# Two layers of linear attention and gated MLP on one core: wider MLP blocks, folded keys for the first tile, and four adjacent tokens to a partition

## The chip, the cores and the metric

The kernel runs on one core of a Trainium2 chip. The metric is the device time of one execution in microseconds, on the slowest core, of which there is one here. The core has five engines that run side by side, each through a fixed sequence of its own: TensorE (PE: matmuls and transposes by matmul; PEld are its weight loads), VectorE (DVE), ScalarE (ACT), GpSimd (POOL) and SyncE (SP, which here only issues transfers). Transfers are carried out by DMA engines that the queues share. Matmuls write to PSUM, everything else lies in SBUF, 128 partitions wide.

## The reference

One sequence of 2048 tokens of width 512 goes twice through the same pair of blocks, with the same weights both times. Type bf16 throughout.

```python
def _A_ref(x, wqkv, w_phi, wo):                      # H = 32 heads of Dh = 16
    qkv = (x @ wqkv).reshape(B, S, 3, H, Dh).transpose(2, 0, 3, 1, 4)
    q, k, v = qkv[0], qkv[1], qkv[2]
    pq = einsum("bhsd,hdf->bhsf", q, w_phi); pk = einsum("bhsd,hdf->bhsf", k, w_phi)
    phi_q = concatenate([softmax(pq), softmax(-pq)]); phi_k = concatenate([softmax(pk), softmax(-pk)])
    kv = einsum("bhsf,bhsd->bhfd", phi_k, v); z = einsum("bhsf->bhf", phi_k)
    o = einsum("bhqf,bhfd->bhqd", phi_q, kv) / (einsum("bhqf,bhf->bhq", phi_q, z)[..., None] + 1e-6)
    return o.transpose(0, 2, 1, 3).reshape(B, S, D) @ wo

def _B_ref(x, W_gate, W_up, W_down):                 # F = 1376
    gate, up = x @ W_gate, x @ W_up
    return ((gate * (gate > 0)) * up) @ W_down

x = A_x
x = x + _A_ref(_layernorm(x), A_wqkv, A_w_phi, A_wo)
x = x + _B_ref(_layernorm(x), B_W_gate, B_W_up, B_W_down)
x = x + _A_ref(_layernorm(x), A_wqkv, A_w_phi, A_wo)
x = x + _B_ref(_layernorm(x), B_W_gate, B_W_up, B_W_down)
```

The sums kv and z run over all tokens, so the queries' part of a layer (`erq` below) cannot begin before the last key of that layer is done.

## The kernel before

**Tiles.** The 2048 tokens are 16 tiles of 128. x stays in SBUF in four chunks X of four tiles each. Token `128 t + p` is on partition p of tile t (`xv` and `ov`, L287 and L288): one partition reads one token, 1 KB, for each tile.

**Start.** ScalarE's queue and SP's queue load x, the key weights wk (into hT_163, in two halves), the value weights wv and the feature weights wf. `chain` (L363) makes each load of a queue follow the one before. Meanwhile nine warm-up matmuls run on TensorE (L445), and one more between two later steps, where IDLE (L173) says so. Since the features of a head are softmax(k wf) with k = x wk, the product wk wf is folded once into Wk2: wcen (VectorE, from wf, L432) and Wblk (a block-diagonal form of it, L433); 16 transposes of wk on TensorE (L471), copied from PSUM to hT_164 (L451 on ScalarE, L452 on VectorE); 16 matmuls with Wblk (L479); four casts into Wk2, 480 columns each (L451, L452). 480 is 32 heads of 15, since the 16th feature follows from the sum.

**Keys and values.** For each tile: statistics on VectorE (L508), a log and an exponential on ScalarE for the deviation (L516, L518), the scaled tile xn (VectorE or GpSimd, L530), a transposition into xnTA (tiles 0 to 3 on TensorE, L498, with a copy at L451 or L452; the others by a transposing transfer that SP issues, L493), then K (four matmuls of 480 columns with Wk2, L600), two exponentials of it (L572), V (four of 512, L605), its copy vext, the sums of the features, their products `ek` (`phi`, VectorE or GpSimd, L559), and the accumulation kvz (L633). With PLAIN = 1 tile 0 takes another path: k = x wk unfolded (KT, 16 matmuls, L591), a copy, then four matmuls with Wblk (L596). It needs neither the transposes of wk nor the folds.

**Queries.** When kvz is complete, VectorE builds R from it (L645, L650). For each tile: Q (L660), exponentials, sums, a ratio, a product `phq` (GpSimd or VectorE, L681) and a transposing transfer fq on SP (L685). `attend` (L690) takes two tiles at a time: erq (eight small matmuls into the one q buffer of PSUM, L696), a reciprocal and the product o on VectorE (L710), the transposing transfer oT on SP (L493), and the output projection (four matmuls of 512, L719), added to x.

**MLP.** `mlp` (L729) works on a block of n tiles: x is centred (xn) and transposed into xnTB by SP (L493). A loop over the ten full f-blocks of 128 makes gate and up, four matmuls each (L796), with n x 128 columns each; narrower blocks take several f-blocks to a PSUM bank (`step = 512 // W`). The last 96 columns of gate and up are made tile by tile (L772) and turned on SP (`hrT`, L823). ScalarE applies the relu (L800); the product hT is made on VectorE, from a copy that ScalarE makes or directly from PSUM. The down projection (L836) has 11 matmuls of 512 columns for each tile; its result is added to x (L843). BLOCKS (L182) gives the widths of the blocks in each layer.

**The order.** Every step is recorded by `op(...)` and runs where a table says: ORDER lists all steps in one sequence, and each engine and each queue runs its own in that sequence; PLACE picks the engine of every step that has two ways (a copy on ScalarE or VectorE, a product on GpSimd or VectorE, a load on SP's or ScalarE's queue); SLOTS names the buffer that each step takes. PSUM has one q buffer and six b buffers. Names such as hT_163 or b_105 are buffers; a number behind the name only tells which.

Of the kernel before, what the change touches and what calls it, by code (L numbers as in the profile page):

```python
# [8 lines left out]
P = 128  # L9
# [136 lines left out]
class K:  # L146
# [9 lines left out]
    "1110001010101011000100001101110100010000110100000001011000010110001111001001000001011100001100001100"  # L156
    "1111010101001111110000100000110110011010010101100000100011000100100000011100111100010000100010111110"
    "1110001011110100001010100000110011100100101001111100101100010101011011111000110100110110100111000100"
    "0010000100011010011111011001000111111100101110100100001"
)  # L160
SLOTS = (
    "0001451040132010500014430222331211020213005544034243050301110131332321832325222114330207421163021150"
    "43375021032559100a020c214d141b332h054f362c105k231i3549013a320g141e203j165b01000000011111020002530110"
    "2052000011050000204202101213001021020100001400010001042032225056210020141101113100001013443103004200"
    "5024102252034024832130232211211001211414305400512015021500501424203120233311431134500254221004105021"
    "02015020100312401021224420100230221701026341142312581332141121113251055111242400k5433334000000400550"
    "4123310521121425400211j0213d222h110f303c033a065k2559325f311d101g145b323g155i002a210c032e260114210204"
    "1100101010020002320110212400001034011022530000104100011021210011114014020514023010050015242135111114"
    "0112013132253124000220001300002341212232511021352150000541521101013132122010250142250053200130123002"
    "05310400520232022520411404202003012523313501311300121120432"  # L170
# [3 lines left out]
    0, 0, 0, 1,  # L174
# [106 lines left out]
def kernel(  # L281
    ctx: ExitStack, tc: tile.TileContext, A_x, A_wqkv, A_w_phi, A_wo, B_x, B_W_gate, B_W_up,
    B_W_down, out):
    nc = tc.nc
    xf, of = A_x.flatten_outer_dims(), out.flatten_outer_dims()
    assert tuple(xf.shape) == (T * P, D)
    xv = xf.rearrange("(t p) d -> p t d", p=P)  # L287
    ov = of.rearrange("(t p) d -> p t d", p=P)  # L288

    sb = ctx.enter_context(tc.tile_pool(name="sb", bufs=1))  # L290
# [72 lines left out]
    def chain(makers):  # L363
        made = []
        for make in makers:
            made.append(make(made[-1:]))
# [588 lines left out]
```

## Time and profile before

| what | value |
|---|---|
| median of 3 runs | 369.92 us (369.61, 369.94, 369.92) |
| the profiled execution's own time | 369.7 us |
| its span, first to last recorded instruction | 367.9 us |
| granted TensorE clock, mean over the span | 1.000 |
| TensorE instructions (matmuls) | 2845 |

The busy shares by slice (40 slices of 9.2 us; 9 means 90% or more) show where each engine works:

```profile
PE   8999999999999999999999999998999999999996
DVE  6999999999886656656799897896874553353415
ACT  5999999343554731356665576863612354212231
POOL 3769931100010000011002172120000000000000
```

The first six slices are the keys of layer 0, with all four engines at work; the keys of layer 1 are made between the MLP blocks of layer 0. The 1.8 us between the span and the execution's time lie outside the recorded instructions.

In the profile's groups of instructions a row reads: line, engine, operation, what it writes <- what it reads, shape, count | busy time, mean ns of one | idle time of the engine just before them, and what ended most of it. In the chain of work that ended last, a row reads: start, length, engine or transfer, buffer, line, count.

### The profile page before, as it was taken

Reading aid. Unit: us, or ns where it says so; the run is one execution under the profiler, and the core shown is the slowest. Engines: PE = TensorE matmul, PEld = TensorE weight load, DVE = VectorE, ACT = ScalarE, POOL = GpSimd, SP = SyncE. Lnnn points to the kernel's source line nnn. Section 1 sums busy time; section 2 is a strip of 40 time slices with the busy share of each in tenths; the row PEclk is TensorE's granted clock in tenths of the full one; section 3 lists DMA queues with packets and bytes.
Section 4 is the critical chain, followed back from the end, with each engine's and each line's share of the span. In section 5 each row is a group of like instructions: output and inputs, shape, how many; then the busy total and the mean of one; then the engine's idle time right before and its main releaser. Section 6 shows DMA issues by size and latency. Waiting matters only on the chain.

```text
span 367.9 us, 7455 instructions
## 1 busy us (share of the span) xinstructions
PE 362.1 (98%) x2845; PEld 217.1 (59%) x2845; DVE 264.5 (72%) x617; ACT 196.6 (53%) x561; POOL 56.6 (15%) x84
## 2 busy tenths in 40 slices
PE   8999999999999999999999999998999999999996
PEld 5455568786554544465767456786654544456674
DVE  6999999999886656656799897896874553353415
ACT  5999999343554731356665576863612354212231
POOL 3769931100010000011002172120000000000000
PEclk9999999999999999999999999999999999999999
DMA  7992983488416302122202350245961220110222
GB/s 229 244 244 64 328 135 61 113 107 178 87 43 116 71 13 18 29 44 58 66 0 66 58 117 7 52 88 78 149 139 25 57 43 2 43 45 0 88 58 87
DMA packets 93924, 31.73 MB, mean 86 GB/s; under 512 B 85344, under 2 KB 92864, under 8 KB 93888
## 3 DMA queue, kind: packets, MB, share of 16 engines
q1 hardware_dynamic: 93616, 31.00, 39.0%
q8 instruction: 22, 0.36, 0.4%
q10 hardware_dynamic: 272, 0.26, 0.2%
q14 instruction: 14, 0.11, 0.1%
HBM read 8.44 MB, written 2.10 MB: 29 GB/s over the span
## 4 chain that ended last, share of the span: by engine, by line
PE 96%; DMA 1%; ACT 1%; DVE 0%; issue 0%
PE b L796 38%; PE b L836 20%; PE b L719 8%; PE b L605 7%; PE b L660 7%; PE b L600 6%; PE b L772 3%; PE q L696 2%; PE q L633 2%; DMA oT<-o 1%; PE q L445 1%; PE b L498 1%; ACT ek L572 1%; PE b L479 0%; PE b L471 0%; DVE X L843 0%
## 5 line engine op out<-in xcount | busy, mean ns | idle before, releaser
L796 PE MATMUL b<-xnTB,wgu 128*128 128x128 bf16 (+2 forms) x1200 | 152.1, 279 | 0.0
L796 PEld LDWEIGHTS <-wgu 128*128 128x128 bf16 x1200 | 97.7, 98 | 46.5
L800 ACT ACTIVATE gu<-b 128x512 bf16<-128x512 f32 (+1 forms) x83 | 47.5, 581 | 93.9 <-PE b L796 85.3
L836 PE MATMUL b<-wd,hT 128*128 128x512 bf16 (+3 forms) x363 | 84.6, 372 | 0.0
L572 ACT ACTIVATE ek<-b 128x480 bf16<-128x480 f32 x128 | 69.4, 587 | 16.2 <-PE b L660 7.7
L813 DVE TENSOR_TENSOR hT<-gu,b 128x512 bf16<-128x512 bf16 (+1 forms) x46 | 30.9, 676 | 33.3 <-PE b L796 19.4
L836 PEld LDWEIGHTS <-hT 128*128 128x128 bf16 (+1 forms) x363 | 34.3, 98 | 33.9
L559 POOL TENSOR_TENSOR ek<-ek 128x480 bf16<-128x480 bf16 x33 | 32.9, 1023 | 127.0 <-ACT sq L670 56.4
L843 DVE SCALAR_TENSOR_TENSOR X<-b,rsB,X 128x512 bf16<-128x512 f32 (+2 forms) x33 | 24.0, 731 | 21.9 <-PE b L836 21.9
L665 DVE TENSOR_REDUCE sq<-ek 128x64 f32<-128x960 bf16 x32 | 36.4, 1143 | 1.3 <-ACT ek L572 1.2
L610 DVE TENSOR_REDUCE sk<-ek 128x64 f32<-128x960 bf16 x32 | 35.8, 1139 | 0.0
L719 PE MATMUL b<-wo,oT 128*128 128x512 bf16 x128 | 31.7, 379 | 1.3 <-DMA oT<-o 1.2
L605 PE MATMUL b<-wv,xnTA 128*128 128x512 bf16 x128 | 31.5, 379 | 0.0
L600 PE MATMUL b<-Wk,xnTA 128*128 128x480 bf16 x124 | 29.5, 366 | 0.6 <-ACT vext L451 0.6
L660 PE MATMUL b<-Wq,xnTA 128*128 128x480 bf16 x128 | 29.7, 366 | 0.0
L804 DVE TENSOR_TENSOR hT<-gu 128x512 bf16<-128x512 bf16 (+1 forms) x37 | 14.8, 401 | 18.0 <-ACT gu L815 17.8
L815 ACT CAST gu<-b 128x512 bf16<-128x512 f32 (+1 forms) x37 | 20.2, 555 | 12.3 <-PE b L796 12.3
L710 DVE TENSOR_TENSOR o<-q,rd 128x512 bf16<-128x512 f32 x32 | 22.0, 687 | 5.8 <-ACT rd L707 5.5
L723 DVE SCALAR_TENSOR_TENSOR X<-b,X 128x512 bf16<-128x512 f32 x32 | 21.8, 684 | 3.8 <-PE b L719 3.6
L508 DVE BATCH_NORM_STATS2 bstA<-X 128x6 f32<-128x512 bf16 x32 | 21.6, 682 | 1.5 <-DMA X<-in_A_x_dram 1.3
L681 POOL TENSOR_TENSOR ek<-ek 128x480 bf16<-128x480 bf16 x13 | 12.9, 994 | 51.3 <-DVE ek L676 48.0
L719 PEld LDWEIGHTS <-oT 128*128 128x128 bf16 x128 | 11.8, 98 | 13.4 <-DMA oT<-o 1.9
(80 smaller groups left out, 339.3 us busy)
## 6 DMA issues: line engine op xcount, KB each, us to landing
out_dram<-X SPq DMA_DIRECT2D x15, 128.0 KB, 1.8
X<-in_A_x_dram SPq DMA_DIRECT2D x6, 256.0 KB, 4.9
wgu<-in_B_W_up_dram SPq DMA_DIRECT2D x4, 344.0 KB, 4.1
wgu<-in_B_W_gate_dram SPq DMA_DIRECT2D x4, 344.0 KB, 5.3
wd<-in_B_W_down_dram SPq DMA_DIRECT2D x5, 256.0 KB, 3.7
hT<-in_A_wqkv_dram SPq DMA_DIRECT2D x3, 256.0 KB, 4.5
X<-in_A_x_dram SPq DMA_DIRECT2D x4, 128.0 KB, 3.3
wv<-in_A_wqkv_dram SPq DMA_DIRECT2D x2, 256.0 KB, 4.8
```

The costliest lines, as they stand in the source:

```text
L559: e.tensor_tensor(out=v[:, :, 0:DF, :], in0=v[:, :, 0:DF, :], in1=spread(ek, v, n), op=Alu.mult)
L572: nc.scalar.activation(out=pairs(ek, s)[:, :, 0:DF, :], in_=ps.t[:, 0:FW].rearrange("p (b f h) -> p b f h", h=2, f=DF), func=AF.Exp, scale ...
L600: k = op("PE", mm(4, FW), due, lambda: [nc.tensor.matmul(kp.t[:, 0:FW], lhsT=xnTA[c][:, i, b, :], rhs=Wk2[:, b, :], start=(b == 0), stop=( ...
L605: v = op("PE", mm(4, 512), due_v, lambda: [nc.tensor.matmul(vp.t[:], lhsT=xnTA[c][:, i, b, :], rhs=wv[:, b, :], start=(b == 0), stop=(b == ...
L610: a = op("DVE", SUM16, due, lambda: nc.vector.tensor_reduce(out=sk.t[:, row, :].rearrange("p (b h) -> p b h", h=2), in_=summed(pairs(ek)), ...
L660: q = op("PE", mm(4, FW), due, lambda: [nc.tensor.matmul(qp.t[:, 0:FW], lhsT=xnTA[c][:, i, b, :], rhs=Wq2[:, b, :], start=(b == 0), stop=( ...
L665: a = op("DVE", SUM16, due, lambda: nc.vector.tensor_reduce(out=sq.t[:].rearrange("p (b h) -> p b h", h=2), in_=summed(pairs(ek)), axis=AX ...
L719: a = op("PE", mm(4, 512), due + 3, lambda j=j, yp=yp: [nc.tensor.matmul(yp.t[:], lhsT=oT.t[:, j, b, :], rhs=wo[:, b, :], start=(b == 0), ...
L796: nc.tensor.matmul(ps.t[:, q * W:(q + 1) * W].rearrange("p (i t) -> p i t", t=P), lhsT=wgu[:, s, b, g * P:(g + 1) * P], rhs=xT.t[:, 0:n, b ...
L800: nc.scalar.activation(out=gu.t[:, 0, 0:cols], in_=gp.t[:, 0:cols], func=AF.Relu)
L813: nc.vector.tensor_tensor(out=h.t[:, f0 * W:f0 * W + cols], in0=gu.t[:, 0, 0:cols], in1=up.t[:, 0:cols], op=Alu.mult)
L836: nc.tensor.matmul(yp.t[:, 0:c1 - c0], lhsT=h.t[:m, f * W + i * P:f * W + (i + 1) * P], rhs=wd[:m, f, c0:c1], start=(f == 0), stop=(f == N ...
```

## The change

Four things change.

- MLP blocks are 1, 1, 2, 4, 4 and 4 tiles in both layers; the last four tiles of layer 0 were two blocks of 2, those of layer 1 blocks of 2, 1 and 1.
- Tile 0's keys are made with the folded weights Wk2 as all others; KT, its copy and the four matmuls with Wblk go.
- Tokens are laid out anew: token `512 c + 4 p + i` is on partition p of tile 4c + i, in x and in the output alike. A load of two tiles then reads 2 KB in one piece for each partition. Since the sums run over all tokens and everything else is done for each token, the result is the same.
- The loads at the start no longer follow one another by rule, those of wv and wf may take either queue, and ORDER, PLACE, SLOTS and IDLE are new: IDLE puts its one warm-up matmul a step later.

```diff
-PLAIN = 1
-BLOCKS = ((1, 1, 2, 4, 4, 2, 2), (1, 1, 2, 4, 4, 2, 1, 1))
+BLOCKS = ((1, 1, 2, 4, 4, 4), (1, 1, 2, 4, 4, 4))
...
 IDLE = (
-    0, 0, 0, 1,
+    0, 0, 0, 0, 1,
 )
...
-    xv = xf.rearrange("(t p) d -> p t d", p=P)
-    ov = of.rearrange("(t p) d -> p t d", p=P)
+    xv = xf.rearrange("(c p i) d -> c p i d", c=C, i=C)
+    ov = of.rearrange("(c p i) d -> c p i d", c=C, i=C)
...
     def load_x(t, n, due, follow=(), eng="SP"):
-        o = load(due, X[t // C][:, t % C:t % C + n, :], xv[:, t:t + n, :], n * 131072, eng, follow, t < 1)
+        o = load(due, X[t // C][:, t % C:t % C + n, :], xv[t // C][:, t % C:t % C + n, :], n * 131072, eng, follow, t < 1)
...
-    def chain(makers):
-        made = []
-        for make in makers:
-            made.append(make(made[-1:]))
-        return made
-
     def w_load(w, k, b, eng):
-        return lambda f: load(b, w[:, b:b + 2, :], wqkv[:, b:b + 2, k * D:(k + 1) * D], 262144, eng, f, w is wk)
+        return lambda f: load(b, w[:, b:b + 2, :], wqkv[:, b:b + 2, k * D:(k + 1) * D], 262144, eng, f, True)
...
-    a0, a1, _ = chain([first_x(0, 1, "ACT"), w_load(wk, 1, 2, "ACT"), lambda f: op(
-        "ACT", (1300, 1300), 5, lambda: nc.scalar.preload_act_table_set("natural_log_exp_and_others"), name="tbl",
-        follow=f)])
-    b0, l_wf, b1, b2, *_ = chain([
-        w_load(wk, 1, 0, "SP"),
-        lambda f: load(2, wf[:], A_w_phi.rearrange("(b j) d f -> (j d) b f", b=NB, j=8), 65536, "SP", f, True),
-        w_load(wv, 2, 0, "SP"), w_load(wv, 2, 2, "SP"), first_x(1, 1), first_x(2, 1), first_x(3, 1), first_x(4, 2),
-        first_x(6, 2), first_x(8, 2), first_x(10, 2), first_x(12, 2), first_x(14, 2)])
-    l_wk, l_wv = [b0, a1], [b1, b2]
+    op("ACT", (1300, 1300), 5, lambda: nc.scalar.preload_act_table_set("natural_log_exp_and_others"), name="tbl")
+    first_x(0, 1)(())
+    l_wv = [w_load(wv, 2, b, "SP")(()) for b in (0, 2)]
+    for t in range(1, 4):
+        first_x(t, 1)(())
+    l_wf = load(2, wf[:], A_w_phi.rearrange("(b j) d f -> (j d) b f", b=NB, j=8), 65536, both=True)
+    l_wk = [w_load(wk, 1, b, "SP")(()) for b in (0, 2)]
+    for t in range(4, T, 2):
+        first_x(t, 2)(())
...
-            if self.l == 0 and t < PLAIN:
-                kT, tp = Buf(p_gu), Buf(p_b)
-                k = op("PE", (960, 1130, 16), due, lambda: [nc.tensor.matmul(
-                    tp.t[:, e * P:(e + 1) * P], lhsT=wk[:, b, e * P:(e + 1) * P], rhs=xnTA[c][:, i, b, :],
-                    start=(b == 0), stop=(b == NB - 1)) for e in range(NB) for b in range(NB)],
-                    [xT] + l_wk, [tp], name="KT")
-                k = evac("DVE", due, lambda: kT.t[:, 0, :], lambda: tp.t[:], [k], [kT], [tp], "kT")
-                k = op("PE", mm(4, 128), due, lambda: [nc.tensor.matmul(
-                    kp.t[:, b * HB * DF:(b + 1) * HB * DF], lhsT=kT.t[:, 0, b * P:(b + 1) * P], rhs=Wblk[:, b, :],
-                    start=True, stop=True) for b in range(NB)], [k, c_blk], [kp], [kT], name="K")
-            else:
-                k = op("PE", mm(4, FW), due, lambda: [nc.tensor.matmul(
-                    kp.t[:, 0:FW], lhsT=xnTA[c][:, i, b, :], rhs=Wk2[:, b, :], start=(b == 0), stop=(b == NB - 1))
-                    for b in range(NB)], [xT] + k_fold, [kp], name="K")
+            k = op("PE", mm(4, FW), due, lambda: [nc.tensor.matmul(
+                kp.t[:, 0:FW], lhsT=xnTA[c][:, i, b, :], rhs=Wk2[:, b, :], start=(b == 0), stop=(b == NB - 1))
+                for b in range(NB)], [xT] + k_fold, [kp], name="K")
...
-                        out=ov[:, t, c0:c1], in_=x_of(t)[:, c0:c1]), [a], name="store",
+                        out=ov[t // C][:, t % C, c0:c1], in_=x_of(t)[:, c0:c1]), [a], name="store",
```

Lines of the changed kernel are some 8 to 19 lower than those of the same code before: K is L581, V L586, Q L641, erq L677, the output projection L700, gate and up L777, down L817, SP's transpositions L485, fq L666, loads L351.

How the order moves, at three places. First the start of SP's queue, which issues most of the first loads. Before (hT_163 holds wk, X_61 to X_64 are the chunks of x):

```order
L353 DMA X_61<-in_A_x_dram 128x512 x3
L353 DMA wf<-in_A_w_phi_dram 128x4x16
L353 DMA hT_163<-in_A_wqkv_dram 128x2x512
L353 DMA X_62<-in_A_x_dram 128x2x512
L353 DMA wv<-in_A_wqkv_dram 128x2x512
L353 DMA X_61<-in_A_x_dram 128x512
L353 DMA wv<-in_A_wqkv_dram 128x2x512
L353 DMA X_64<-in_A_x_dram 128x2x512
L353 DMA X_62<-in_A_x_dram 128x2x512
L353 DMA X_63<-in_A_x_dram 128x2x512
```

And in the changed kernel:

```order
L351 DMA X_61<-in_A_x_dram 128x512
L351 DMA hT_163<-in_A_wqkv_dram 128x2x512
L351 DMA X_61<-in_A_x_dram 128x512
L351 DMA X_62<-in_A_x_dram 128x1024
L351 DMA hT_163<-in_A_wqkv_dram 128x2x512
L351 DMA X_61<-in_A_x_dram 128x512
L351 DMA wv<-in_A_wqkv_dram 128x2x512 x2
L351 DMA X_62<-in_A_x_dram 128x1024
L351 DMA X_63<-in_A_x_dram 128x1024
L351 DMA X_64<-in_A_x_dram 128x1024
```

Both halves of wk are on SP's queue now, the second behind a pair of x tiles; before, ScalarE's queue issued one of them. ScalarE's queue issues one tile of x and then wf instead.

Second, ScalarE's instructions in the same stretch, in which the copies to hT_164 and the casts to Wk make the folded weights. Before:

```order
L451 COPY xnTA_79<-b_105 128x512
L518 ACTIVATE rsA_89<-lnA_90 128x1
L451 COPY hT_164<-b_107 128x4x128
L451 CAST Wk_67<-b_103 128x480
L451 COPY hT_164<-b_108 128x4x128
L451 CAST Wk_67<-b_104 128x480
L516 ACTIVATE lnA_90<-mvA_88 128x2
L451 CAST gu_165<-b_105 128x512
L518 ACTIVATE rsA_89<-lnA_90 128x2
L451 CAST Wk_67<-b_107 128x480
L516 ACTIVATE lnA_90<-mvA_88 128x1
L451 CAST Wk_67<-b_103 128x480
```

In the changed kernel:

```order
L508 ACTIVATE lnA_90<-mvA_88 128x1
L443 COPY hT_164<-b_103 128x4x128
L443 COPY hT_164<-b_104 128x4x128
L508 ACTIVATE lnA_90<-mvA_88 128x1
L510 ACTIVATE rsA_89<-lnA_90 128x1 x2
L443 COPY xnTA_79<-b_105 128x512
L443 CAST Wk_67<-b_106 128x480
L508 ACTIVATE lnA_90<-mvA_88 128x2
L443 COPY hT_164<-b_107 128x4x128
L510 ACTIVATE rsA_89<-lnA_90 128x2
L443 CAST Wk_67<-b_103 128x480
L443 CAST Wk_67<-b_106 128x480
```

ScalarE makes three of the four copies to hT_164 and three of the four casts to Wk, VectorE the others (before, ScalarE made all eight); the copies stand behind a log that needs tile 1's statistics (which on VectorE now come behind wcen, and so behind wf), and the copy of tile 0's plain keys (gu_165) is gone. Wblk has moved to GpSimd, behind tile 0's xn.

Third, SP's queue where the queries of layer 1 begin. Before:

```order
L685 DMA_TRANSPOSE fq_148<-ek_121 128x8x128
L493 DMA_TRANSPOSE oT_158<-o_157 128x8x128
L685 DMA_TRANSPOSE fq_147<-ek_127 128x8x128
L685 DMA_TRANSPOSE fq_146<-ek_125 128x8x128
L823 DMA_TRANSPOSE hT_164<-hr_171 128x1x128
L493 DMA_TRANSPOSE oT_160<-o_156 128x8x128
L493 DMA_TRANSPOSE xnTB_162<-xn_110 128x8x128
L493 DMA_TRANSPOSE oT_159<-o_157 128x8x128
```

In the changed kernel:

```order
L666 DMA_TRANSPOSE fq_148<-ek_130 128x8x128
L485 DMA_TRANSPOSE oT_160<-o_157 128x8x128
L804 DMA_TRANSPOSE hT_163<-hr_170 128x1x128
L485 DMA_TRANSPOSE oT_158<-o_156 128x8x128
L485 DMA_TRANSPOSE xnTB_161<-xn_109 128x8x128
L666 DMA_TRANSPOSE fq_151<-ek_123 128x8x128
L666 DMA_TRANSPOSE fq_147<-ek_127 128x8x128
L804 DMA_TRANSPOSE hT_164<-hr_171 128x1x128
L666 DMA_TRANSPOSE fq_150<-ek_124 128x8x128
L485 DMA_TRANSPOSE oT_159<-o_157 128x8x128
```

The second oT stood behind two fq and an hT; it stands directly behind an hT, and the two fq have gone behind it and behind xnTB.

More of the change, by code (lines that the diff above doesn't have):

```diff
@@ L155 @@
 PLACE = (
[L156 to L159, printed above, removed]
+    "1001001010001001101010000101111000001001111100100001101100111011000011000000100000101111011100010100"
@@ L160 @@
+    "1001101111010010110000010110000011011001111010011101100111110011110011001111111010011101111101011001"
+    "1100011011011000110101111111111101111110010101011000010100100001101000100101111100010011011001010100"
+    "1010110010011111000100110101101001100101100011101100100"
 )
 SLOTS = (
-    "0001451040132010500014430222331211020213005544034243050301110131332321832325222114330207421163021150"
-    "43375021032559100a020c214d141b332h054f362c105k231i3549013a320g141e203j165b01000000011111020002530110"
@@ L169 @@
-    "0112013132253124000220001300002341212232511021352150000541521101013132122010250142250053200130123002"
-    "05310400520232022520411404202003012523313501311300121120432"
+    "0001450332111040002521331020252213134130241204554001324122142118332305232454002133223601357001146113"
+    "37331110214c1029215b124e344a030f050d1609305j031g253c321b012i144h204k360a1200050401151502000212011020"
+    "2400001150000020350210121400102105010002500401004005212214201851002313115213501425303231310500410142"
+    "1024202011521574410443221121100401010352431312302242101240511013402460230322025003051301002510502000"
@@ L171 @@
+    "1042222135013132244254224011350135402481030275405k21311041150211321401210232450232222330131532542063"
+    "2110112025213310385404e052f313d2459131i320j201b062b154f210c145a3509160h004d212e331g12011301020313001"
+    "0124302000035011021540000124501002145001012230210000111041011030210121231001501441322200001041042225"
+    "0420351321112001514214224324413412402523105223205102100110050000220551450552131532232412541321040123"
+    "1130421000550542551212451342421030015034"
 )
```

5 lines of the change are left out of this document (removed), and 179 rows, old and new, of the table ORDER.

## The prediction

> **What bounds the kernel now.** I read the page first (span, shares, the chain that ended last), then the same chain piece by piece in order of time, then what TensorE waited for. From the page:
>
> ```profile
> span 367.9 us, 7455 instructions
> ...
> PE 362.1 (98%) x2845; PEld 217.1 (59%) x2845; DVE 264.5 (72%) x617; ACT 196.6 (53%) x561; POOL 56.6 (15%) x84
> ...
> PE 96%; DMA 1%; ACT 1%; DVE 0%; issue 0%
> ```
>
> TensorE carries 96% of the chain. The pieces below (start, length, what, how many instructions) give the pace of each kind of matmul and the places where the chain leaves TensorE:
>
> ```profile
> 0.77 4.00 PE q L445 x9
> ...
> 7.72 0.42 PE b L479 x8
> ...
> 15.87 0.97 PE b L600 x4
> ...
> 97.61 4.32 PE b L796 x20
> ...
> 245.90 4.92 DMA oT<-o
> ...
> 253.68 1.75 PE b L796 x16
> ...
> 356.56 4.47 PE b L796 x80
> ```
>
> So a 512-column matmul costs 4.32/20 = 0.216 us, a 256-column one 1.75/16 = 0.1094, a 128-column one 4.47/80 = 0.0559. Twice 0.1094 is 0.2188 and four times 0.0559 is 0.2236: a narrower matmul costs almost in proportion, plus about 2.4 ns for each instruction. The nine warm-up matmuls take 0.44 us each, twice the later cost; at 7.72 the pace is full (0.42/8 = 0.0525 for 120 columns): the array starts at half speed and leaves it between, near 6.5. The longest wait of TensorE (total, times, longest):
>
> ```profile
> PE b L719 <- DMA oT<-o: 1.2, 1, 1.2
> ```
>
> The time is therefore the sum of the matmuls, a start in which they are late, a wait near 246 (and one near 15, below), and a tail.
>
> **Wider blocks.** In layer 0 two blocks of two tiles become one of four: 160 matmuls of 256 columns (17.50 us) become 80 of 512 (17.28). In layer 1 blocks of 2, 1, 1 become one of four: 80 of 256 and 160 of 128 (8.75 + 8.94 = 17.69) become 80 of 512 (17.28). Gate and up gain 0.22 + 0.41 = **0.63 us**, all on the path. The down projections and the last 96 columns keep their matmuls.
>
> [...]
>
> **Keys of tile 0.** The plain path goes. What TensorE did up to the wait at 15.87, and its pieces at the start:
>
> ```profile
> L605 PE MATMUL b<-wv,xnTA 128*128 128x512 bf16 x12 | 3.1, 378 | 0.0
> L600 PE MATMUL b<-Wk,xnTA 128*128 128x480 bf16 x12 | 2.9, 366 | 0.0
> L498 PE MATMUL b<-ident,xn 128*128 128x128 bf16 x16 | 1.8, 244 | 0.2 <-DVE xn L532 0.2
> L471 PE MATMUL b<-ident,hT 128*128 128x128 bf16 x16 | 1.7, 267 | 0.0
> L479 PE MATMUL b<-Wblk,hT 128*128 128x120 bf16 x16 | 1.2, 216 | 0.0
> L591 PE MATMUL b<-xnTA,hT 128*128 128x128 bf16 x16 | 1.1, 219 | 0.0
> L596 PE MATMUL b<-Wblk,gu 128*128 128x120 bf16 x4 | 0.4, 216 | 0.0
> ```
>
> ```profile
> 8.14 0.89 PE b L591 x16
> ...
> 9.68 0.97 PE b L605 x4
> 10.65 0.21 PE b L596 x4
> ...
> 11.73 0.82 PE b L600 x4
> ```
>
> L591 and L596 (0.89 + 0.21 = 1.10) leave; four matmuls of L600's kind come (0.81, the 0.82 row). That is **0.29 us** less work.
>
> But the plain path was what TensorE did while the folded weights were being made. The useful work in the group rows, at full pace, is 12 x 0.216 + 12 x 0.204 + 48 x 0.056 + 20 x 0.0525 = 8.8 us (warm-up not counted). At 15.87 TensorE is thus 15.87 - 8.8 = 7.1 us late. The same sum for the changed order needs the moment at which the first K can start. The rows for it:
>
> ```profile
> 2.12 0.43 SPq L353 DMA_DIRECT2D wf<-in_A_w_phi_dram  x1
> ...
> 4.79 0.77 POOL L530 TENSOR_SCALAR xn<-X,nm,rsA 128x512 bf16<-128x512 bf16 x1 [0.35 <-POOL nm L528]
> ...
> 7.10 0.45 PEld L471 LDWEIGHTS <-hT 128*128 128x128 bf16 x8 [0.21 <-DMA hT<-in_A_wqkv_dram]
> ...
> 7.24 0.41 DVE L452 COPY xnTA<-b 128x512 bf16<-128x512 bf16 x1
> ...
> 7.76 1.29 DVE L508 BATCH_NORM_STATS2 bstA<-X 128x6 f32<-128x512 bf16 x2
> ...
> 15.86 0.52 PEld L600 LDWEIGHTS <-xnTA 128*128 128x128 bf16 x4 [1.08 <-DMA xnTA<-xn]
> ```
>
> And, from the list of transfers up to 12 us (KB each, median us to landing) and from the groups by line:
>
> ```profile
> X<-in_A_x_dram SPq DMA_DIRECT2D x4, 256.0 KB, 5.3
> ...
> hT<-in_A_wqkv_dram ACTq DMA_DIRECT2D x1, 256.0 KB, 3.2
> ...
> wf<-in_A_w_phi_dram SPq DMA_DIRECT2D x1, 16.0 KB, 4.1
> ```
>
> ```profile
> L559 POOL TENSOR_TENSOR ek<-ek 128x480 bf16<-128x480 bf16 x33 | 32.9, 1023 | 127.0 <-ACT sq L670 56.4 <-ACT ek L622 43.9 <-DVE ek L559 26.8
> ...
> L452 DVE CAST vext<-b 128x512 bf16<-128x512 f32 x7 | 4.7, 682 | 0.5 <-PE b L605 0.5
> ```
>
> Two chains run into the first K. One begins with wf, now the second transfer of ScalarE's queue, issued near 1.2 us (after one issue of the length of the row's 0.43); with the 4.1 us of the row it lands at 5.3. VectorE waits for it with the second tile's aggregate behind it, and ScalarE's log and then both copies of hT wait for that. Wblk, moved to GpSimd, has no row there; its bounds are 0.41 us (a VectorE operation of its size, the copy row) and the 1.02 us of GpSimd's 480-column products, to which it is nearest; behind xn (to 5.56) it ends at 6.6, before the copies do. The other chain begins with the second half of wk, the fifth transfer on SP as before, but with one more pair of x tiles (256 KB) ahead of it: 7.1 becomes about 7.5 (0.7 if the added bytes move at the pace at which 256 KB pieces land later, 0 if the gap that wf left in the stream is filled). Then eight transposes (0.45), the copy, x statistics of one tile (0.65) and a copy (0.41) ahead of the last cast on VectorE (0.68), with two folds between: the last Wk2 is there near 10.9, and the first K starts at about **11.0**. By then the useful work is 28 transposes, 16 folds and one V, 28 x 0.056 + 16 x 0.0525 + 0.86 = 3.3 us; TensorE is 7.7 us late, 0.6 more than before at 15.87. The wait at 15.87, which is inside the 7.1, should not come back: its xnTA transposition is the same length, and four K and four V now stand ahead of its reader, where there were three and three. So the start costs **+0.6 us**. Bounds: K directly behind the V that the last piece of wv allows (9.7 + 0.86) gives +0.2; K at 12.5, if either chain slips by 1.5 us (the landings of the neighbours spread from 3.2 to 5.3), gives +2.1. I take the worked value.
>
> The second piece of layout, x in 2 KB runs for pairs of tiles, moves the same bytes; I give it nothing. Its bounds are a gain of the 0.4 us that the extra pair costs wk above, and no loss, since single tiles keep 1 KB runs; the stores too.
>
> **The waits later.** The wait at 250.86 began on SP's queue:
>
> ```profile
> 241.94 2.58 SPq L685 DMA_TRANSPOSE fq<-ek  x2
> ...
> 245.90 1.26 SPq L493 DMA_TRANSPOSE oT<-o  x1
> ```
>
> Four transpositions stand back to back, the first held by its late fq, and oT lands 4.9 us after issue instead of the usual 3.2 (next row).
>
> ```profile
> DMA to landing us min/median/max: 3.1/3.2/4.9
> ```
>
> ```profile
> L710 DVE TENSOR_TENSOR o<-q,rd 128x512 bf16<-128x512 f32 x32 | 22.0, 687 | 5.8 <-ACT rd L707 5.5
> ```
>
> In the changed order this oT stands directly behind an hT, ahead of the two fq and of xnTB. I remove the **1.25 us**. The next oT stands behind fq, fq, hT, fq instead; the matmuls between its erq and its reader are 6.8 us, against some 1.4 for o (0.69 for the product, as much for what comes before it), up to 1.3 of queue and 3.2 to 4.9 of transfer: between none and 0.8 lost; I take 0.25. Another wait is new: between the last kvz of layer 1 and the first erq stood eight Q matmuls, now four.
>
> ```profile
> 226.37 1.78 PE L660 MATMUL b<-Wq,xnTA 128*128 128x480 bf16 x8
> ...
> 227.18 0.18 DVE L650 SCALAR_TENSOR_TENSOR R<-q,Mg 128x32 bf16<-128x32 f32 x1
> ```
>
> R ends at 227.36, and four Q from 226.37 end at 227.18: **0.25 us** with the hand-over.
>
> **What stays hidden.** Many products and copies change engine. The order has 12 more phi products on GpSimd, 12 fewer on VectorE, five value copies moved from ScalarE to VectorE. The one stage where that could bite:
>
> ```profile
> 20.00:60.00 40.00, 40.00 (x360) 22.64 (x358) 38.26 (x69) 38.87 (x119) 26.88 (x30) 1.00 0.70 176
> ```
>
> VectorE and ScalarE have under 2 us of 40 free; five casts less (5 x 0.6) help ScalarE, five more and twelve products less leave VectorE no worse. GpSimd has 13 us free for 12 us of products. TensorE's full 40 us is the cover; without it each late cast would be paid in full. The tail (last down, last addition, last store) has the same 384 and 128 columns at its end. One warm-up matmul stands one step later, its cost as before.
>
> **Sum.** 369.7 - 0.63 - 0.29 + 0.6 - 1.25 + 0.25 + 0.25 = 368.6 for an execution like the profiled one. That one lies 0.2 us below the median of the runs shown, 369.92, so the forecast is 0.2 higher: **368.8 us**.
>
> **Rivals.** *The wait only moves.* Another oT or xnTA is late by as much, as one was in the old order although by the order 8.4 us of matmuls covered it. Then the 1.25 stays: 370.0. For it speaks that SP's queue is in order and just as full; against it, that the waits show one such wait for all the oT of two layers. *The start is late (slower).* wf, split into short runs, is now on a second queue beside full loads; if it or the second half of wk lands 2.4 us after my estimate, K starts at 13.4, TensorE has nothing else (all later K need the same Wk2), and the time is 371.2. It decides from K at about 12.9, since 1.9 us more turn the forecast into 0.2% slower. For it: the spread of landings, and that VectorE and ScalarE both queue behind wf. Against: wf's 4.1 us were measured with three loads ahead of it on its queue, and now there is one. *The clock falls back.* The half pace lasted 5.7 us, from 0.77 to near 6.5; a second such stretch after the gaps near 7 and 9 us would cost 2.9 us, 371.7. The 1.08 us gap before 15.87 did not do it: four K follow in 0.97. [...] *More gain.* Wider runs of x and a filled stream bring K at 10.5 and no new waits: 367.8. [...]
>
> **How the numbers follow.** My case 0.50, its own range 368.0 to 369.6; wait moves 0.20; late start 0.16; clock 0.03; more gain 0.10; page 0.01. About 0.2% (0.74 us) is what a measurement here tells from no change: faster means under 369.2, slower over 370.7. Faster: 0.37 of my case, 0.10, 0.03 and 0.01, **0.51**. Same: 0.13 of mine and 0.15 of the moved wait, **0.28**. Slower: 0.16, 0.03 and 0.02, **0.21**. The range, 367.1 to 371.2, goes down to more gain with half a microsecond and up to the late start.
>
> **What would show it.** Right: 960 gate and up matmuls at unchanged pace; first L581 (K) at 10.5 to 11.6; no wait on oT above 0.5; a short idle before the first erq of layer 1. Wrong: K after 12.5, an oT or xnTA wait above 1 us, half pace after 7 us, or VectorE or ScalarE ending TensorE's idle time between 20 and 60.

## The result, and the profile after

| | before | changed |
|---|---|---|
| median, 22 runs each | 369.75 us (369.32 to 370.30) | 368.87 us (368.40 to 370.13) |
| ratio to before, 95% interval | | 0.9978 (0.9971 to 0.9984) |
| profiled execution: time, span | 369.7, 367.9 us | 368.89, 367.1 us |
| last matmul ends (modelled) | 364.95 us | 362.52 us |
| from there to the span's end | 2.93 us | 4.59 us |

The changed kernel is faster by 0.8 to 0.9 us, and the forecast of 368.8 lies beside it. The last two rows say that the sum was met in another way than forecast: TensorE is done 2.4 us earlier, and 1.7 us of that are given back behind its last matmul.

From the page of the changed kernel (span, busy time, the chain's shares by engine, the gate and up matmuls):

```profile
span 367.1 us, 6928 instructions
...
PE 360.5 (98%) x2589; PEld 199.2 (54%) x2589; DVE 267.8 (73%) x607; ACT 188.2 (51%) x530; POOL 71.4 (19%) x101
...
PE 93%; DMA 3%; DVE 2%; issue 0%; ACTq 0%; SPq 0%; ACT 0%
...
L777 PE MATMUL b<-xnTB,wgu 128*128 128x512 bf16 (+2 forms) x960 | 150.7, 308 | 0.0
```

The start, in order of time (start, length, engine, line; the number in brackets is idle time and what ended it):

```profile
4.79 0.28 DVE L414 TENSOR_TENSOR wd<-wf 128x120 bf16<-128x120 bf16 x1
...
5.69 1.01 POOL L419 TENSOR_TENSOR Wblk<-wd,Mf 128x480 bf16<-128x480 bf16 x1
...
6.97 0.45 PEld L463 LDWEIGHTS <-hT 128*128 128x128 bf16 x8
...
8.98 0.62 DVE L444 CAST Wk<-b 128x480 bf16<-128x480 f32 x1
...
9.06 1.03 PE L586 MATMUL b<-wv,xnTA 128*128 128x512 bf16 x4
...
9.92 1.78 PE L581 MATMUL b<-Wk,xnTA 128*128 128x480 bf16 x8
```

wf is used at 4.79, the second half of wk at 6.97, the last cast ends at 9.60, and the first K stands directly behind the first V, at 9.92: nothing keeps it waiting. What TensorE waited for behind its first matmul (total, times, longest):

```profile
PE b L490 <- POOL xn L522: 0.5, 1, 0.5
PE b L471 <- ACT rsA L510: 0.4, 1, 0.4
PE q L614 <- DVE ek L551: 0.3, 1, 0.3
```

All three lie before 20 us; no transfer is waited for later. Where the first erq of layer 1 waits for R:

```profile
225.62 0.97 PE L641 MATMUL b<-Wq,xnTA 128*128 128x480 bf16 x4
226.67 0.41 PE L677 MATMUL q<-R,fq 128*128 128x68 bf16 x8
```

Four Q take 0.81 at their pace and end at 226.43; erq starts 0.24 later. The stage in which VectorE and ScalarE are fullest (window; then busy time of PE, PEld, DVE, ACT, POOL; clock, DMA share, GB/s):

```profile
20.00:60.00 40.00, 40.00 (x361) 22.74 (x359) 38.56 (x71) 39.05 (x120) 26.54 (x31) 1.00 0.75 184
```

TensorE still covers it, though the two now have under 1.5 us of 40 free. Last the tail of the changed kernel, in four views: VectorE's last instructions in time, SP's queue in time, what SP waited for (total, times, longest), and the transfers from 364.1 to 365.2 with the last store's size and us to landing:

```profile
361.94 0.97 DVE L824 SCALAR_TENSOR_TENSOR X<-b,rsB,X 128x384 bf16<-128x384 f32 x2 [0.39 <-PE b L817]
```

```profile
351.37 1.19 SPq L804 DMA_TRANSPOSE hT<-hr  x1
357.69 6.47 SPq L890 DMA_DIRECT2D out_dram<-X  x13
```

```profile
SPq L890 <- DVE X L824: 14.4, 3, 9.1
```

```profile
q14 instruction: 1, 0.01, 5.3%
issues: line engine op xcount, KB each, median us to landing
out_dram<-X SPq DMA_DIRECT2D x1, 32.0 KB, 2.3
```

The last piece of x is ready at 362.91. SP is then near the end of 13 stores issued back to back from 357.69 to 364.16: it had waited 5.0 us for the data of the first of them, the store of tile 13, and behind it stood those of tiles 3, 0, 6, 1 and 7, which had long been ready. (The 9.1 us of the view are at an earlier store, that of tile 9, issued at 347.95; the expectation of experiment 1 puts them at tile 13.) The last store goes out at 363.75, 0.84 us after its data, and takes 2.25 us to land. Before, it went out after 0.10 and landed after 1.50:

```profile
out_dram<-X SPq DMA_DIRECT2D x1, 32.0 KB, 1.5
```

And among the packets of the last store's window is one that is no data: an instruction packet on queue q14.

### The profile page after: what moved, and what is told of

Read it like the earlier page. It is cut to its first block, busy times and chain, and to the rows that moved or that the text cites. A ratio compares the mean times of both kernels' runs of the same rounds, so it can differ in the third digit from the quotient of the medians.

```text
span 367.1 us, 6928 instructions
## 1 busy us (share of the span) xinstructions
PE 360.5 (98%) x2589; PEld 199.2 (54%) x2589; DVE 267.8 (73%) x607; ACT 188.2 (51%) x530; POOL 71.4 (19%) x101
## 4 chain that ended last, share of the span: by engine, by line
PE 93%; DMA 3%; DVE 2%; issue 0%; ACTq 0%; SPq 0%; ACT 0%
PE b L777 38%; PE b L817 21%; PE b L700 8%; PE b L641 7%; PE b L586 6%; PE b L581 6%; PE b L753 3%; PE q L614 2%; PE q L677 2%; DMA X<-in_A_x_dram 2%; DMA wf<-in_A_w_phi_dram 1%; DVE bstA L500 1%; PE b L490 1%; DVE sk L591 1%; DVE X L824 0%
## 5 line engine op out<-in xcount | busy, mean ns | idle before, releaser
L777 PE MATMUL b<-xnTB,wgu 128*128 128x512 bf16 (+2 forms) x960 | 150.7, 308 | 0.0
L777 PEld LDWEIGHTS <-wgu 128*128 128x128 bf16 x960 | 80.3, 98 | 57.4 <-issue 0.2
L817 PE MATMUL b<-wd,hT 128*128 128x512 bf16 (+3 forms) x363 | 84.1, 372 | 0.0
L564 ACT ACTIVATE ek<-b 128x480 bf16<-128x480 f32 x128 | 68.2, 585 | 11.4 <-PE b L641 7.0
L794 DVE TENSOR_TENSOR hT<-gu,b 128x512 bf16<-128x512 bf16 (+1 forms) x53 | 35.1, 663 | 36.3 <-PE b L777 19.8
L551 POOL TENSOR_TENSOR ek<-ek 128x480 bf16<-128x480 bf16 x40 | 39.2, 1008 | 94.2 <-ACT ek L603 93.9
L817 PEld LDWEIGHTS <-hT 128*128 128x128 bf16 (+1 forms) x363 | 34.5, 98 | 37.4
L662 POOL TENSOR_TENSOR ek<-ek 128x480 bf16<-128x480 bf16 x18 | 18.3, 1020 | 87.2 <-DVE ek L657 56.6
L700 PE MATMUL b<-wo,oT 128*128 128x512 bf16 x128 | 31.4, 379 | 0.0
L586 PE MATMUL b<-wv,xnTA 128*128 128x512 bf16 x128 | 31.4, 379 | 0.0
L581 PE MATMUL b<-Wk,xnTA 128*128 128x480 bf16 x128 | 30.2, 366 | 0.0
L641 PE MATMUL b<-Wq,xnTA 128*128 128x480 bf16 x128 | 30.1, 365 | 0.0
L785 DVE TENSOR_TENSOR hT<-gu 128x512 bf16<-128x512 bf16 x29 | 12.1, 421 | 21.0 <-ACT gu L796 21.0
L796 ACT CAST gu<-b 128x512 bf16<-128x512 f32 x29 | 17.0, 586 | 16.2 <-PE b L777 15.4
L700 PEld LDWEIGHTS <-oT 128*128 128x128 bf16 x128 | 12.2, 98 | 13.2
```

The costliest lines, as they stand in the source:

```text
L551: e.tensor_tensor(out=v[:, :, 0:DF, :], in0=v[:, :, 0:DF, :], in1=spread(ek, v, n), op=Alu.mult)
L564: nc.scalar.activation(out=pairs(ek, s)[:, :, 0:DF, :], in_=ps.t[:, 0:FW].rearrange("p (b f h) -> p b f h", h=2, f=DF), func=AF.Exp, scale ...
L581: k = op("PE", mm(4, FW), due, lambda: [nc.tensor.matmul(kp.t[:, 0:FW], lhsT=xnTA[c][:, i, b, :], rhs=Wk2[:, b, :], start=(b == 0), stop=( ...
L586: v = op("PE", mm(4, 512), due_v, lambda: [nc.tensor.matmul(vp.t[:], lhsT=xnTA[c][:, i, b, :], rhs=wv[:, b, :], start=(b == 0), stop=(b == ...
L641: q = op("PE", mm(4, FW), due, lambda: [nc.tensor.matmul(qp.t[:, 0:FW], lhsT=xnTA[c][:, i, b, :], rhs=Wq2[:, b, :], start=(b == 0), stop=( ...
L700: a = op("PE", mm(4, 512), due + 3, lambda j=j, yp=yp: [nc.tensor.matmul(yp.t[:], lhsT=oT.t[:, j, b, :], rhs=wo[:, b, :], start=(b == 0), ...
```

## The experiments

Each was timed beside the kernel before on the same chip; 369.9 to 370.0 there. `moved(ORDER, steps, mark)` is a helper that takes steps out of the order and puts them behind the step `mark`.

**1. The stores moved ahead** (changed kernel, SP's queue alone).

```diff
+ORDER = moved(ORDER, (1576, 1496, 1528, 1666, 1667, 1664, 1665), 1738)
+ORDER = moved(ORDER, (1757, 1758, 1755), 1742)
```

> The changed kernel, with ten stores moved ahead in SP's queue and nothing else: the stores of tiles 3, 0, 1, 6, 7, 4 and 5 directly behind the third block's hr transposition, those of 10, 11 and 8 directly behind the fourth block's. Theory (the order of the stores): in the changed kernel SP waits 9.1 us at the store of tile 13 with stores behind it that had long been ready; 13 issues then run from 357.69 to 364.16, and the last store goes out 0.84 us after its data and lands 2.25 us after issue, where before it took 0.10 and 1.50. With the ready stores gone from there the last matmul stays at 362.5, the last store goes out within 0.2 us of its data and lands in about 1.5, so the span falls by about 1.5 us, to 365.6, and the time to 367.4 (range 367.1 to 367.8). Rival (the layout of the output makes stores slow): only the issue's 0.7 us or less is gained, landing stays above 2.1 us, and the time is 368.2 or more. Rival (nothing at the tail depends on the queue): 368.9.

368.73 us, ratio 0.9973 (0.9961 to 0.9986): next to nothing against the changed kernel. The last store did go out at once, at 363.08 with its data ready at 362.98, but took longer still. Transfers issued from 363 to 363.5, and then what the DMA engines did from 364.1 to 365.0 (40 slices of 22 ns, busy tenths):

```profile
out_dram<-X SPq DMA_DIRECT2D x1, 32.0 KB, 2.7
```

```profile
DMA  6592100000000000000000000000000000000110
...
q14 instruction: 1, 0.01, 5.4%
```

By 364.23 all is written but a rest that comes 0.7 us later. In the packet records 120 of the store's 128 packets are done by then; the other eight, by their number one of 16 DMA engines' share, run from 364.93 to 365.05, and an instruction packet of 8 KB lies from 364.16 to 364.94. By this the store waited behind an engine's instruction fetch; experiment 2 tests it.

**2. The fetch moved as well** (1, and 24 instructions more on VectorE).

```diff
+        for at, o in enumerate(order):
+            if at == 1700:
+                for _ in range(24):
+                    nc.vector.memset(wasteD[:, 0:1], 0.0)
```

> The changed kernel with the stores moved ahead (as in the run of that name) and 24 tiny memsets on VectorE near 310 us, on a scratch tile that nothing reads. Theory (an instruction fetch holds up the last store): in the run with the stores moved the last store went out 0.1 us after its data and still took 2.68 us, and in the list of transfers one instruction packet of 8 KB (queue q14, 0.78 us from 364.16) lies in that time; by its place it belongs to VectorE, whose instruction stream reaches a block's end with its last instructions. 24 instructions more ahead of it let that fetch start near 335 to 347 us; the last store then lands in 1.5 to 1.9 us, the span is 366.0, the time 367.7 (range 367.3 to 368.1). Rival (the fetch is another engine's or comes with the program's end): a fetch stays near 364.2, the last store takes over 2.2 us, 368.7. Rival (the fetch does no harm): the fetch moves, the last store still takes 2.3 us or more, 368.7.

367.65 us, ratio 0.9942 (0.9930 to 0.9954). Transfers from 363.7 to the end:

```profile
q1 hardware_dynamic: 288, 0.13, 14.0%
issues: line engine op xcount, KB each, median us to landing
out_dram<-X SPq DMA_DIRECT2D x1, 32.0 KB, 1.6
```

No instruction packet is left there; a new one lies at 330.47. The fetch was VectorE's, since memsets on VectorE alone moved it from 364.16, and it held up the last store: 2.7 us to landing with it, 1.6 without. This kernel has the lowest median of all that ran (that of 11 cannot be told from it), and it beats both the kernel before and the changed one with intervals that do not touch.

**3. The memsets alone** (stores as in the changed kernel).

> The changed kernel with the 24 memsets on VectorE alone; the stores stay where they were. It parts the two causes of the long tail: the queue (the last store goes out 0.8 us after its data) and the fetch (it lands 2.25 us after issue instead of 1.5). Theory (the two come one after the other, and the fetch alone hides what the queue costs): last store issued near 363.75 again, landing 1.5 to 1.8 us later, 0.6 us less than the changed kernel, 368.25 (368.0 to 368.5). Rival (the fetch alone matters): 367.7. Rival (the queue alone): 368.9.

368.43 us, ratio 0.9965 (0.9952 to 0.9979). The last store goes out 1.05 us after its data and lands in 1.58. By the medians the stores alone gave 0.1 us, the memsets alone 0.4 and both together 1.2, each known to half a microsecond. The profiled executions point the same way: from the last matmul to the span's end it takes 4.59 us in the changed kernel, 4.28 with the stores moved, 4.12 with the memsets, 3.15 with both. While one cause is there, it hides most of the other.

**4. The layout of before in the changed kernel.**

```diff
+    xv = xf.rearrange("(c i p) d -> c p i d", c=C, i=C)
+    ov = of.rearrange("(c i p) d -> c p i d", c=C, i=C)
```

> The changed kernel with x and the output laid out as before (token 128 t + p on partition p of tile t); order, blocks and keys stay changed. Theory (the layout is worth nothing, as the prediction had it): time within 0.2 us of the changed kernel's 368.87, first K at 9.7 to 10.2, the last store lands about 2.2 us after issue as with the new layout. Rival (2 KB runs make the first loads faster): the second half of wk lands 0.4 us or more later than 6.93, K at 10.3 or later, time 369.2 or more. Rival (stores in adjacent tokens are slow): the last store lands in 1.6 us and the time falls to 368.2.

368.71 us, ratio 0.9968 (0.9956 to 0.9980). The second half of wk lands at 7.49 and the first K starts at 10.48, 0.56 later; at the first erq of layer 0 (51.25 us, in the changed kernel 51.27) nothing of it is left. (Single executions: in six with the new layout and the new loads K starts between 9.92 and 10.33.) The last store lands in 2.28 us as with the new layout, but an instruction packet lies in both; without one it lands in 1.53 with the new layout (5) and 1.50 with the old (kernel before). So adjacent tokens do not slow it.

**5. The new layout in the kernel before** (the same two lines in the other kernel).

> The kernel before with the new layout of x and the output, all else as it was. With the old layout in the changed kernel the second half of wk landed at 7.49 instead of 6.9 and wv's second half at 9.35 instead of 8.7, and the time was the same. Theory (loads land 0.4 us earlier, and the later waits of the start take it up): V starts 0.3 to 0.6 us earlier, time within 0.25 us of the kernel before. Rival (the start is the sum of its loads): 0.4 us less or more.

370.56 us, ratio 1.0019 (1.0004 to 1.0035). V starts at 10.12, no earlier than in other executions of the old order (9.63 to 10.45), so the loads gained nothing there. That the time is rather longer I cannot explain; the layout is no gain in either order.

**6. The old widths for the last four tiles** (changed kernel; `parts` are the ranges of tiles that one matmul takes).

```diff
+                parts = ((0, n),) if t0 < 12 else ((0, 2), (2, 4)) if l == 0 else ((0, 2), (2, 3), (3, 4))
...
+                    for i0, i1 in parts:
```

> The changed kernel, with the gate and up matmuls of its last four tiles issued in the widths of before: in layer 0 two of 256 columns for each of 512, in layer 1 one of 256 and two of 128. 240 more matmuls, same data, same order of steps. Theory (the term of the prediction: a narrow matmul costs in proportion plus about 2.4 ns): 0.63 us more, 369.5 (369.3 to 369.7), and 0.0559 us for each of the 128-column ones. Rival (a weight load between narrow matmuls costs more than the matmul hides): over 1.5 us more, 370.4 or later, and a pace of the 128-column matmuls above 0.07 us. Rival (the cost is hidden): 368.9.

370.15 us, ratio 1.0010 (1.0001 to 1.0020): 1.28 more, between theory and rival, and the trace says why. A wait is back, at another oT, which takes 4.86 us instead of 3.24, and in its transfer lies an instruction packet, here on q8 between 283 and 284.5:

```profile
286.20 1.04 PE L700 MATMUL b<-wo,oT 128*128 128x512 bf16 x4 [1.22 <-DMA oT<-o]
```

```profile
q8 instruction: 1, 0.02, 3.9%
```

From the first erq of layer 0 to the last matmul the changed kernel takes 311.25 us and this one 313.23; 1.41 of the 1.98 more lie between the two matmuls around that wait, and 0.57 are left for the 240 extra matmuls, 2.4 ns each. The price was right; the wait is the surprise.

**7. The late oT ahead in SP's queue** (kernel before).

```diff
+ORDER = moved(ORDER, (1402,), 1401)
```

> The kernel before, with one transposition moved in SP's queue: the oT for which TensorE waited 1.25 us at 250.86 goes ahead of the second fq and of hT, behind the first fq. Theory (its place in the queue made the wait): o is ready at 243.16 and the transfer goes out at 243.3 instead of 245.9, lands by 248.3 at the latest, and the wait at 250.86 goes; 1.25 us less, 368.5 (368.2 to 368.8). Rival (the wait only moves): the hT or fq that is now later, or the xnTB behind it, is waited for by as much, 369.4 or more. Rival (the transfer, not the queue, was slow): it takes 5 us or more from issue again because of what else moves at that time; then it still lands by 248.3 and only the theory's reason differs, to be seen in its landing.

369.54 us, ratio 0.9990 (0.9978 to 1.0003). The wait at the oT went, and one as long came at the hT that now stood in its place (third row: its landing):

```profile
PE b L844 <- DMA hT<-hr: 1.3, 1, 1.3
```

```profile
fq<-ek SPq DMA_TRANSPOSE x1, 2.9
hT<-hr SPq DMA_TRANSPOSE x1, 4.7
```

The fq issued just ahead took 2.9, the hT 4.7 where 2.4 is usual: it is not the queue that is slow but something at about 249.7, whatever stands there. The view of the transfers from 249.5 to 251 has an instruction packet on q8.

**8. TensorE's fetch moved** (kernel before; SP's order untouched).

```diff
+            n = 4 if self.l == 0 and t < 8 else 1
...
+                vp.t[:, lo:lo + D // n], lhsT=xnTA[c][:, i, b, :], rhs=wv[:, b, lo:lo + D // n],
...
+                for lo in range(0, D, D // n) for b in range(NB)], [xT] + l_wv, [vp], name="V")
```

> The kernel before, with the V matmuls of tiles 0 to 7 of layer 0 issued as four of 128 columns for each of 512: 96 more matmuls with their 96 weight loads, 0.23 us more by the price of 2.4 ns each, and TensorE's instruction stream 192 instructions longer ahead of everything else; SP's queue stays as it is. Theory (TensorE's instruction fetch made the wait at 250.86): a 16 KB instruction packet (queue q8) lay from 248.81 to 249.77 in the transfer of the oT that was waited for; there is one for every 256 instructions of TensorE, so that 192 more move each to where the stream was 192 instructions earlier, near 245 us here. The oT then lands 3.2 to 4 us after issue instead of 4.9, and the wait at 250.86 falls from 1.25 us to under 0.4; time 368.9 (368.5 to 369.3). Rival (SP's queue made it, as the prediction had it): oT still lands 4.9 us after issue at the same place, wait 1.2 us, time 370.0. Rival (a fetch now hits another transfer that TensorE waits for): the wait at 250.86 goes and one as long stands elsewhere, 370.0.

368.93 us, ratio 0.9972 (0.9960 to 0.9983), although it has 0.23 us of matmuls more. The same oT, in the kernel before and here:

```profile
oT<-o SPq DMA_TRANSPOSE x1, 4.9
```

```profile
oT<-o SPq DMA_TRANSPOSE x1, 3.2
```

In the kernel before one packet of 16 KB lies in its transfer (window 248.6 to 249.9); here the fetches are at 242.72 and 253.69:

```profile
q8 instruction: 1, 0.02, 4.6%
```

Three transpositions were back to back in front of this oT in both. The wait of 1.25 us is gone, so the fetch made it, not the queue.

**9 and 10. The kernel before without the plain path**, and the same with 16 matmuls more (V of four tiles in halves), so that TensorE's stream is as long as before.

```diff
-PLAIN = 1
+PLAIN = 0
```

(Tile 0's K goes behind the second tile's V in the order; the tables lose the entries of the steps that are gone.)

> The kernel before, with tile 0's keys by the folded weights: the 16 matmuls on wk, the copy and the four with Wblk go, four of 480 columns come, and stand behind the V of the second tile. All else stays. Theory (the plain path was cover, not cost): TensorE idles where the 16 matmuls stood, the first K starts at 11.0 to 11.8, and the wait at 15.86, which ends with a transposition's landing, takes up what is left; the time stays within 0.25 us of the kernel before, though 0.29 us of matmuls are gone. Rival (the plain path cost its matmuls): 0.3 us less or more than that. Rival (it hid the folds fully): the first K later than 12.2, 0.5 us more.

> The kernel before without the plain path for tile 0, as in the run of that name, but with the V matmuls of tiles 0 to 3 of layer 0 in two halves of 256 columns: 16 matmuls more, so that TensorE's instruction stream is as long as in the kernel before again. In the run without them the time was that of the kernel before (369.82), but there the wait at 250.86 was gone too, since 32 instructions less had moved TensorE's fetch from 248.8 to 252.7. Theory (the plain path hid about 1.2 us, and the moved fetch paid that back): with the count restored the fetch lies in the oT transfer again, the wait of 1.2 us is back, and the time is 371.0 (370.6 to 371.4). Rival (the plain path was worth nothing and the fetch has no part in it): 369.9.

369.82 us, ratio 0.9993 (0.9984 to 1.0003), and 370.27, ratio 1.0004 (0.9993 to 1.0016). First K at 11.70 and 12.19. In the first the oT wait is gone and the fetch stands at 252.74; in the second both are back, the fetch at 249.74 and the oT taking 4.9 us:

```profile
PE b L721 <- DMA oT<-o: 1.2, 1, 1.2
```

So 32 instructions of TensorE, taken away and put back, take the wait away and bring it back, as in 8. The times differ by 0.45 and not by the 1.2 that I expected, so what else differs between the two stays open. With the fetch where it was, dropping the plain path costs 0.15 us, with an interval from 0.3 less to 0.6 more, though 0.29 us of matmuls are gone. That fits cover that cost nothing; a loss of 1.2 us it rules out.

**11. Two more waits** (2, and two steps moved on TensorE).

```diff
+ORDER = moved(ORDER, (63,), 275)
+ORDER = moved(ORDER, (1313,), 1304)
```

> The changed kernel with the stores moved ahead, the 24 memsets, and two steps moved on TensorE: the first kvz of layer 0 behind the next fold and V (it waited 0.3 to 0.5 us for VectorE's product at 19.45), and one more Q ahead of the first erq of layer 1 (which waited 0.23 us for R). Theory: both waits go, 0.6 us less than with the memsets alone, 367.1 (366.7 to 367.6). Rival (the work behind is late by as much and the waits move): same as with the memsets alone.

367.76 us, ratio 0.9951 (0.9934 to 0.9968): a miss. TensorE waits neither for the first kvz's product nor for R; instead it waits 0.5 us for the product o, two steps further on.

**12. Another place for TensorE's fetch** (2, V of four tiles in quarters).

> The changed kernel with stores moved and memsets, and the V matmuls of tiles 0 to 3 of layer 0 in four of 128 columns: 48 more matmuls, 0.12 us, and TensorE's fetches 96 instructions earlier. In the run without it a fetch at 238.05 lay in an oT transfer that took 4.73 us, and TensorE waited 0.36 us for it. Theory: that wait goes, 0.25 us less, 367.4 (367.1 to 367.8). Rival (a fetch hits another transfer that is waited for): 367.8 or more.

368.37 us, ratio 0.9957 (0.9943 to 0.9970): the rival. The oT wait is gone, and a fetch at 208.87 now lies in the transfer of an xnTA for the keys of layer 1, which takes 4.87 us instead of the 2.73 in 2; TensorE waits for it at 211.66:

```profile
PE b L590 <- DMA xnTA<-xn: 0.9, 1, 0.9
```

## Why the prediction was right

The time, the sign and the range were right; but three of its terms were wrong, and their errors cancelled. That the time came out within 0.1 us is luck.

- *Bound.* TensorE sets the time (93% of the chain that ended last), and gate and up run at the old pace: in experiment 6 the trace gives 0.57 us for the 240 matmuls, forecast 0.63. No run shows narrow matmuls that cost far more than their columns, for which the last of the chances, 0.01, stood: the extra ones of experiment 6 cost 2.4 ns each.
- *Keys of tile 0.* Four K for 20 other matmuls, as forecast; in the old order, without the new one's loads, dropping the plain path gained nothing that could be measured (9 and 10). Which of the new loads, copies and casts makes up for its cover in the changed kernel was not tested apart; the layout does not (4).
- *Start, +0.6.* Wrong. K started at 9.92, not at 11.0, and so ahead of the 10.5 to 11.6 that were named as a sign of being right. Both chains were sized too long: wk's second half landed at 6.93 instead of 7.5, wf at 4.77 instead of 5.3, and from wk's landing to the last Wk2 it took 2.7 us (to 9.60) instead of 3.4. What K stood behind was V, the prediction's lower bound. (Wblk on GpSimd took 1.01, the upper of its two bounds.) Counting idle time of TensorE up to 57 us, both profiled executions are equally late: the term is 0 and not 0.6. (The 1.08 us that the prediction read at 15.87 are the wait of the weight load; the matmuls stood still for 0.62.) The yardstick was also an early one: in five profiled executions of the old loads V starts between 9.63 and 10.45, in the one read for the prediction at 9.63.
- *The oT wait, −1.25.* The size was right, 1.4 from matmul to matmul; the reason was wrong. "Four transpositions stand back to back" was true, but experiment 7 took the oT out of the row and the wait passed to its successor, and experiment 8 left the row and took the fetch away. The changed kernel has some 200 instructions of TensorE less ahead of this place (256 matmuls and as many weight loads less in all), and its fetches fall elsewhere (245.06 and 258.13 instead of 248.81), where they hold up no transfer that is waited for: the oT that the first of them overlaps lands in 3.08 us. Whether its order of SP's queue helps too was not shown.
- *The next oT, +0.25.* It did not come: no oT is waited for, and some 0.4 us of smaller waits of TensorE (one of 0.2 at 124.1 in the kernel before and others) went too.
- *R, +0.25.* Right: 0.24, at the place named.
- *The tail, 0.* Wrong, and the largest error: +1.66 in the profiled execution, of which 0.74 is the later issue, 0.75 the slower landing and the rest lies behind the landing. The step that failed is that the tail "has the same 384 and 128 columns at its end": I looked at the matmuls and not at what stands on SP's queue ahead of the last store. The fetch could not be read from the order, but the ready stores behind a late one could.
- *Hidden work.* Right: no idle time of TensorE between 20 and 60, as the windows show.
- *The clock falls back.* This rival did not come in the profiled execution, where TensorE has its full clock from 4.66 us on. But it exists: in the profiled execution of experiment 3 half pace came back from 7.85 to 11.27 (granted clock 0.50), the first K started at 11.78, and the time was 369.99 against the median of 368.43. What set it off was not shown: TensorE was busy for 1.89 of the 3.41 us before, and its longest wait there was 0.7. Of ten executions on record with a mean granted clock of 0.992 to 0.995, four of them of the kernel before, nine took 1.1 to 2.0 us more than their median and one 4.8; the prediction's price was 2.9.

Against the forecast of 368.6 for an execution like the profiled one, the start gave 0.6 back and the waits 0.8 (0.25 for the next oT, 0.4 smaller ones, 0.15 more at the oT itself), and the tail took 1.7; what is left is the 0.3 by which that execution was over it. Up to the last matmul the terms add up as measured: 0.57 for the blocks, 0.29 for the keys, 1.4 and 0.4 for the waits, less 0.24 for R, are the 2.4 us of the table.

## What to carry to other kernels

When a store or a transposition is late by about a microsecond for no reason in its queue, look among the transfers for an instruction packet: a change of a few dozen instructions ahead on the same engine moves it (24 memsets on VectorE one from 364.16 to 330.47, 32 instructions of TensorE one from 249.74 to 252.74), and the time can go with it (1.1 us less from experiment 1 to 2), so compare two orders of a kernel only after looking where these packets fall. On an in-order queue put every store that is ready ahead of the first that will wait, above all near the end (here the last store went out 0.84 us after its data). And follow the last output to its landing: a saving on the engine that bounds the kernel counts only up to there: of 2.4 us here, 1.7 were given back behind the last matmul.

## What the runs showed of the hardware

Instruction fetches can hold up data transfers. TensorE's come as packets of 16 KB on q8, 22 in the kernel before and 20 in the changed one, with 257 of its recorded instructions between two of them in the mean (222 to 284), and last 0.9 to 1.9 us; the others are of 8 KB on q14, 0.3 to 1.0 us as a rule, VectorE's among them (the one that the memsets of experiment 2 moved). In the 14 traces of this study an oT issued behind 40 us took 3.12 us in the median and never over 3.38 when no fetch overlapped it (141 of them), and 4.16 in the median, up to 5.22, when one did (61); 28 of the 61 were no longer than the others, so a fetch does not hold up all that it meets. TensorE shows no wait for its own fetches: the view of its waits in the changed kernel has none behind 20 us, with 19 of them there. The transfer beside a fetch can be late: the oT of the kernel before took 4.9 us instead of 3.2, for which TensorE waited 1.25, and the last store of the changed kernel 0.75 us more than before.
